# Spectra taken back one slot later, and an output projection in whole tiles with split operands

## The chip, the cores and the metric

The kernel runs on one core of a Trainium2 chip. The metric is the device time of one execution in microseconds (us), as the median of several runs. TensorE is called PE here, its weight loads PEld, VectorE DVE, ScalarE ACT, GpSimd POOL and SyncE SP. All transfers between memory and the core's buffers are issued from SP.

## What is computed

Two layers work on 2048 positions of 448 channels, and their results stand side by side in the output.

```python
# left half: a long convolution per channel (S4D), done with Fourier transforms
dt = exp(log_dt);  A = -exp(log_A_real) + 1j * A_imag;  C = (C_real + 1j * C_imag) * dt[:, None]
P = exp((A * dt[:, None])[:, :, None] * arange(L)[None, None, :])      # D x N x L, N = 256
K = 2.0 * einsum("dn,dnl->dl", C, P).real
y = irfft(rfft(u_t, 2 * L) * rfft(K, 2 * L))[:, :, :L];  a = y.T + u * D_skip
# right half: full attention, 16 heads of 28 channels
q, k, v = split(x @ wqkv)
b = (softmax(q @ k.T * 28 ** -0.5) @ v).reshape(S, D) @ wo
out = concatenate([a, b], axis=-1)
```

## The kernel before, in words

**Attention.** The 16 heads lie in four groups of four heads, and the 2048 queries in four blocks of 512. A unit is one group and one block, so there are 16 units, numbered 0 to 15; units 12 to 15 are the last group. A unit walks over 16 blocks of 128 keys. Each of these 256 pairs (unit u, key block kt) is one step `s` of the main loop (line 1006). For each step there are four score matmuls (`s_mm`: PE writes `pss`, ACT writes the exponentials `p`), four times two column-tiled matmuls with the values of the step before (`pv_step`, tile `po`) and, as long as there is a unit one ahead, four matmuls for the row maxima of that unit (`max_mm`, reduced on DVE). The row maxima end 19 steps before the loop does.

**Order of the work.** `ORDER` (line 34) writes out the order within a step: maximum and score matmuls, then a slot `f`, the value matmuls `pv`, a second slot `f`, and the rest of the maximum and score matmuls. All engines keep program order from here on (line 864), so an instruction that waits holds up all that is behind it on its engine. From step 238 on, each step has a third slot at its end. After the loop there are only slots, two to a step number.

**Slots.** `slot` (line 957) hands each slot to the first that is due: the sums, the scaling and the row maxima of a unit (`urgent`), output projections (`p_due`), matmuls of the convolution kernel (`m_due`), transforms of the input (`u_due`), and otherwise the jobs of the convolution's end (`f_slot`). From step 256 on spectra go ahead of projections. The jobs are:

- 16 spectra (`spectrum`, line 776; halves f = 0 and 1, eight each). Tasks: `forth(0)`; `forth(1)` with two products on DVE each and then `join(0)`, `join(1)`, four sums and differences on POOL, tile `p`; `back(0)` and `back(1)`, PE matmuls on `p`, followed by a copy on ACT and a store `z`. `back(0)` may come only `GAP` slots after `forth(1)`. One spectrum runs at a time; the next one's data (`mw`, `yk`, `uh`) are loaded when one begins.
- 8 pieces of finish (`finish`, line 819; four per half, after all spectra of that half). A load of `zi` and `ut`, a product on POOL, and four matmul groups with an addition on DVE (`one`), stored in pairs.

The second half of the spectra waits until the convolution kernel is done (step 200, lines 1013 to 1017), when the memory and a PSUM bank of that work are given to the ring of four `pm` tiles that all slots use. The first slots of the spectra lie at step 195.

**End of a unit.** `fin` (line 734) copies `po` to `o`, and slots for the row sums (`sums`) and for the scaling follow two and four slots later. In `scale`, PE spreads the reciprocals and DVE multiplies into `on`. For units 0 to 11 `on` is stored (`on_d`); for 12 to 15 four projections of 128 queries each become due, one per step, from two steps after `fin` on. `project` multiplies the four groups' outputs by Wo in float32 through `mm32`, which cuts a 128-column weight into four column tiles of 32; a float32 matmul is two records in the trace. The outputs of the first three groups come as `og` in one load at kt = 12 of the unit (line 1018). Wo lies in two tiles that take both buffers named `ua` (`load_wo`, line 704), so rows that show `pm<-ua,og` and `pm<-ua,on` are projections. ACT copies the result to `y`, which is stored. Rows `pm<-yk,mw` are forth, `pm<-p,mw` back, `p<-pr,pr` join, `pm<-zi,wb` finish.

Every record of the trace carries line 75, the helper through which all instructions are issued, so groups are told apart by their tiles. Matmul operands of type float32r go through PE as one record with whole tiles. Queries, keys and the value projection use that type already, with each operand split into a high part (a rounding copy on ACT) and a rest (a subtraction).

Of the kernel before, what the change touches and what calls it, by code (L numbers as in the profile page):

```python
# [8 lines left out]
F32 = mybir.dt.float32  # L9
F32R = mybir.dt.float32r  # L10
I32 = mybir.dt.int32
AF = mybir.ActivationFunctionType
ALU = mybir.AluOpType
# [5 lines left out]
D = 448  # L19
# [3 lines left out]
G = 4  # L23
HG = H // G
CQ = 512
NQ = L // CQ
# [4 lines left out]
NU = G * NQ  # L31
# [2 lines left out]
ORDER = ('m0', 's0', 'm1', 's1', 'v', 'f', 'pv', 'f', 'v', 'k', 'm2', 's2', 'm3', 's3', 'v')  # L34
PB = 8
F1 = 2
FX, PD, GAP = 1, 2, 2
FL = {"s": 2, "f": 3}
S0, SP, SW, SD, PW, E3 = 0, 4, 0, 5, 37, 8
UG = (2, 2, 4)  # L40
# [50 lines left out]
def body(ctx, tc, a, out):  # L91
    nc = Engines(tc)
# [4 lines left out]
    def pool(stack, name, bufs=1, space=None, side=None):  # L97
        kw = {} if space is None else {"space": space}
        if side:
            kw["side"] = side  # L100
        return stack.enter_context(tc.tile_pool(name=name, bufs=bufs, reuse_waits="tile", **kw))
# [11 lines left out]
    on_d = [dram.tile([G, 128, CQ], F32, name=f"on_{c}") for c in range(NQ)]  # L113
# [11 lines left out]
    def w_tile():  # L125

        n_ring[0] += 1
        return ps_w[0].tile([128, CQ], F32, name=f"pm{n_ring[0] % ps_w[1]}")
# [7 lines left out]
    def mm32(o, w, x_, start, stop, at=0):  # L136

        for i in range(w.shape[-1] // 32):
            c = slice(32 * i, 32 * i + 32)
            nc.tensor.matmul(o[c], w[:, c], x_, start=start, stop=stop, tile_position=(0, at + 32 * i))  # L140
# [4 lines left out]
    def load_k(g, j, p):  # L145
        if j == 0:
            t = k0_t if g == 0 else p.tile([128, HG, L], F32R, name="khat")
            kt_g[g] = [t[:, i] for i in range(HG)]
        for r in range(4):
            nc.sync.dma_start(kt_g[g][j][32 * r:32 * r + 32, :].bitcast(F32), k_d[g][r % 2, 32 * j:32 * j + 32, :])  # L150
# [3 lines left out]
    def load_v(g, c):  # L154
        v_g[g, c] = t = v_p.tile([128, NK // NQ, HG, 32], F32, name="v", bufs=5)
        nc.sync.dma_start(t.rearrange("p t h e -> p t (h e)"), v_d[c][:, g])

    def load_kd(g, j, rows=range(4)):
        if 0 in rows:
            kd_g[g, j] = kd_p.tile([128, CQ], F32R, name=f"kdif{j}")  # L160
        t = kd_g[g, j]
        for r in rows:
            nc.sync.dma_start(t[32 * r:32 * r + 32].bitcast(F32), kd_d[g][r % 2, 32 * j:32 * j + 32, :])

    def load_q(u, rows=range(4)):
        g, c = divmod(u, NQ)
        if 0 in rows:
            q_u[u] = q_p.tile([128, HG, CQ], F32R, name="qhat", bufs=3)
        t = q_u[u]
        for r in rows:  # L170
            nc.sync.dma_start(t[32 * r:32 * r + 32].bitcast(F32), q_d[g][c][r // 2].rearrange("(j p) q -> p j q", j=HG))
# [40 lines left out]
    with ExitStack() as st:  # L212
# [47 lines left out]
        t = a["A_log_dt"]  # L260
# [10 lines left out]
        for k in range(NCK):  # L271
            for s in (1, 0):
                src = wns[k][:, s, :].rearrange("p (g h e) -> p g h e", g=G, e=DH)
                hi, lo = (w_g[:, i, s, k, :, :, :DH] for i in range(2))
# [280 lines left out]
    kq_p = pool(kq_st, "kq_p")  # L555
# [146 lines left out]
    wo_t = []  # L702
# [11 lines left out]
    def s_mm(u, kt, j):  # L714
        pss = ps_s.tile([128, CQ], F32, name="pss")
        nc.tensor.matmul(pss, kt_g[u // NQ][j][:, kt * 128:(kt + 1) * 128], q_u[u][:, j, :], start=True, stop=True)
        p = kq_p.tile([128, CQ], F32, name="p", bufs=PB)
        nc.scalar.activation(p, pss, AF.Exp, scale=SCALE)
        return p
# [5 lines left out]
            nc.tensor.matmul(o_u[u][32 * j:32 * j + 32, :], v_g[u // NQ, kt // NQ][:, kt % NQ, j, :], ps[j],  # L725
                             start=kt == 0, stop=kt == NK - 1, tile_position=(0, 32 * j))

    og_u = {}

    def load_og(u):  # L730
        og_u[u] = og = kq_p.tile([128, G - 1, CQ], F32, name="og")
        nc.sync.dma_start(og, on_d[u % NQ][:G - 1].rearrange("g p q -> p g q"))

    def fin(u, s_):
        g, c = divmod(u, NQ)
        o = kq_p.tile([128, CQ], F32, name="o")
        nc.scalar.activation(o, o_u[u], AF.Copy)
        on = kq_p.tile([128, CQ], F32, name="on", bufs=2)
        rb = kq_p.tile([128, 4, HG, 32], F32, name="rb")
        og = og_u.pop(u, None)  # L740

        def sums():
            pw = w_tile()
            for t in range(4):
                mm32(pw[:, t * HG:(t + 1) * HG], o[:, t * 128:(t + 1) * 128], sel, start=True, stop=True)
            r = kq_p.tile([128, 4, HG], F32, name="r", bufs=2)
            nc.vector.reciprocal(r, pw[:, :4 * HG].rearrange("p (t h) -> p t h", h=HG))
            nc.scalar.activation(rb, r[:, :, :, None].to_broadcast([128, 4, HG, 32]), AF.Copy)

        def scale():  # L750
            pw = w_tile()
            for t in range(4):
                mm32(pw[:, t * 128:(t + 1) * 128], rb[:, t].rearrange("p h e -> p (h e)"), ident, True, True)
            nc.vector.tensor_tensor(on, o, pw, ALU.mult)
            if g < G - 1:
                nc.sync.dma_start(on_d[c][g], on)
            else:
                p_due.extend((s_ + PD + PS * t, lambda t=t: project(t)) for t in range(4))

        def project(t):  # L760
            pw = w_tile()
            ts = slice(t * 128, (t + 1) * 128)
            for g2 in range(G):
                mm32(pw[:, :D], og[:, g2, ts] if g2 < G - 1 else on[:, ts], wo_t[g2 // 2][:, g2 % 2, :],
                     start=g2 == 0, stop=g2 == G - 1)
            y = kq_p.tile([128, D], F32, name="y", bufs=2)
            nc.scalar.activation(y, pw[:, :D], AF.Copy)
            q0 = c * CQ + t * 128
            nc.sync.dma_start(out[q0:q0 + 128, D:], y)

        soon_slot(UG[1], sums)
        soon_slot(UG[2], scale)

    fk = {}
# [130 lines left out]
    f0_st, f1_st = ExitStack(), ExitStack()  # L905
    f_p, f_ready = {}, {}
# [43 lines left out]
    def soon_slot(gap, f):  # L950
        n_urgent[0] += 1
        urgent.append((n_slot[0] + gap, n_urgent[0], f))
        q = sorted(urgent)
        urgent.clear()
        urgent.extend(q)
# [45 lines left out]
    def vec():  # L1001
        if powers["g"]:
            powers["g"].popleft()()

    prev = None
    for s in range(NS):
        u, kt = divmod(s, NK)
        sm = s + NK + LEAD
        if s == 12 * NK:
            k0_st.close()  # L1010
            f_p["s", 0] = f_p["s", 1] = pool(f0_st, "f0_p", side="right")
            f_ready["s", 0], f_ready["s", 1] = s, NS
        if s >= 12 * NK and f_ready["s", 1] == NS and not (k_due or m_due or powers["g"] or powers["e"]):
            g_st.close()
            ps_st.close()
            ps_w[:] = pool(ps_st, "ps_f", 4, PSUM), 1
            f_ready["s", 1] = s + F1
        if kt == 12 and u // NQ == G - 1:
            load_og(u)
        late[0] = s + NK + LEAD > NS  # L1020
        if u % NQ == NQ - 1 and u < NU - 1 and kt % 4 == 2:
            load_v(u // NQ + 1, kt // 4)
        if sm < NS and sm // NK % NQ == NQ - 1 and sm % NK % 4 == 0 and sm % NK and sm // (NQ * NK) + 1 < G:
            load_kd(sm // (NQ * NK) + 1, sm % NK // 4 - 1)
        if sm < NS and sm % (NQ * NK) == 0 and sm:
            load_kd(sm // (NQ * NK), HG - 1)
        if kt % 4 == 1 and u % NQ == 1 and u // NQ + 1 < G:
            load_k(u // NQ + 1, kt // 4, k_pools[(u // NQ + 1) % 2])
        if kt == 2:
            if u + 2 < NU:  # L1030
                load_q(u + 2)
        ps = []
        for op in ORDER:
            if op[0] == "s":
                ps.append(s_mm(u, kt, int(op[1])))
            elif op[0] == "f":
                slot(s)
            elif op[0] == "v":
                vec()
            elif op == "k":  # L1040
                k_next()
                k_begin(s)
                k_seed(s)
                for _ in range(3):
                    if powers["e"]:
                        powers["e"].popleft()()
            elif op == "pv":
                if prev:
                    pv_step(*prev)
                    if prev[1] == NK - 1:  # L1050
                        fin(prev[0], s)
            elif sm < NS:
                max_mm(sm // NK, sm % NK, int(op[1]))
        for _ in range(FX if late[0] else 0):
            slot(s)
        if sm < NS and sm % NK == NK - 1:
            def end(un=sm // NK):
                max_end(un, w_tile())
                max_put(un)
            max_join(sm // NK)  # L1060
            soon_slot(UG[0], end)
        k_next()
        prev = (u, kt, ps)
    pv_step(*prev)
    fin(prev[0], NS)
    s = NS
# [63 lines left out]
```

## Time and profile before

| | us |
|---|---|
| median of 3 runs | 1319.46 |
| lowest and highest | 1316.6, 1322.87 |
| profiled execution | 1316.79 |
| its span, first to last instruction | 1315.1 |
| PE busy | 1229.7 |
| DVE, ACT, POOL busy | 948.6, 953.0, 870.4 |

Mean granted PE clock over the span is 0.98 of full speed. Unit 12 begins at step 192, and the last values' matmul of the loop is at 1292.9 us. In rows of time order the first number is the start in us from the span's start, the second the duration, then engine, line, operation, written tile, read tiles, shape and count; brackets hold the idle time before and what ended it. In lists of waits the numbers are the total in us, the times, and the longest. In rows of groups they are the count, then busy us and mean ns of one, then idle time before. A list of transfers gives their count and KB each.

### The profile page before, as it was taken

How to read it: one execution, taken by the hardware profiler on the slowest of the kernel's cores; microseconds unless marked ns; L12 is line 12 of the kernel's file. 1: busy time of each engine (PE TensorE's matmuls, PEld its weight loads, DVE VectorE, ACT ScalarE, POOL GpSimd, SP SyncE). 2: the span in 40 equal slices, each digit the busy share in tenths (PEclk: the TensorE clock that was granted, in tenths of full speed). 3: DMA queues.
4: the chain of work that ended last, by engine and by line, in shares of the span. 5: the costliest groups of instructions: out<-in, count | busy, mean ns of one | idle time of the engine just before them, and what ended most of it. 6: DMA issues, size and time to landing. Idle time of an engine off the chain costs nothing.

```text
span 1315.1 us, 33199 instructions
## 1 busy us (share of the span) xinstructions
PE 1229.7 (94%) x12625; PEld 698.8 (53%) x12625; DVE 948.6 (72%) x2106; ACT 953.0 (72%) x2068; POOL 870.4 (66%) x736
## 2 busy tenths in 40 slices
PE   6879985899999999999999999999999899999897
PEld 4657763455555555555555555555555444544333
DVE  5898887878777777778778888888887545645111
ACT  4876762488888888888788888888887656646453
POOL 3686681398887788887779999989993414423311
PEclk9989987899999999999999999999999999999999
DMA  6677769736765546468633233732416553925485
GB/s 190 206 276 260 242 205 285 220 73 143 179 147 132 129 136 175 131 174 224 167 100 87 61 78 90 161 80 70 101 37 175 178 158 132 284 87 186 132 219 137
DMA packets 200087, 205.35 MB, mean 156 GB/s; under 512 B 95992, under 2 KB 158520, under 8 KB 197880
## 3 DMA queue, kind: packets, MB, share of 16 engines
q1 hardware_dynamic: 199928, 203.23, 55.9%
q8 instruction: 100, 1.64, 0.5%
q14 instruction: 59, 0.48, 0.1%
HBM read 120.73 MB, written 82.18 MB: 154 GB/s over the span
## 4 chain that ended last, share of the span: by engine, by line
PE 71%; DVE 9%; POOL 7%; DMA 5%; ACT 4%; issue 4%; SPq 0%; ACTq 0%; POOLq 0%; DVEq 0%
PE pm L75 40%; PE pss L75 16%; PE po L75 15%; POOL p L75 2%; DMA k<-hl 2%; DVE tri L75 2%; POOL e L75 1%; DVE mx L75 1%; POOL qhat L75 1%; DVE sg L75 1%; ACT tri L75 1%; DVE px L75 1%; DVE qhat L75 1%; DMA khat<-k 1%; ACT p L75 1%
## 5 line engine op out<-in xcount | busy, mean ns | idle before, releaser
L75 ACT ACTIVATE p<-pss 128x512 f32<-128x512 f32 x1024 | 560.9, 610 | 112.3 <-PE pss L75 109.1
L75 DVE TENSOR_REDUCE mx<-pm 128x1 f32<-128x512 f32 x500 | 321.7, 684 | 125.5 <-PE pm L75 123.4
L75 PE MATMUL pss<-qhat,khat 128*128 128x512 f32 x1024 | 403.3, 400 | 2.3 <-ACT p L75 2.3
L75 PE MATMUL pm<-khat,qhat 128*128 128x512 f32 x749 | 327.1, 440 | 3.4 <-DVE mx L75 2.3
L75 POOL TENSOR_TENSOR e<-e,sdb 128x256 f32<-128x256 f32 x168 | 202.1, 1203 | 118.4 <-ACT e L75 63.1
L75 PE MATMUL po<-p,v 128*32 128x512 f32 x2048 | 269.8, 595 | 0.0
L75 POOL TENSOR_TENSOR e<-e,eu 128x256 f32<-128x256 f32 x168 | 248.3, 1478 | 13.2
L75 PEld LDWEIGHTS pm<-khat,qhat 128*128 128x128 f32 x749 | 141.9, 190 | 197.3 <-ACT p L75 41.9
L75 DVE CUSTOM_DVE_ANT_0 rl<-pm,rl 128x512 f32<-128x512 f32 x249 | 171.5, 689 | 64.8 <-ACT rl L75 61.8
L75 PEld LDWEIGHTS pss<-qhat,khat 128*128 128x128 f32 x1024 | 191.1, 189 | 49.0 <-issue 12.2
L75 POOL TENSOR_TENSOR eu<-e,sdb 128x256 f32<-128x256 f32 x168 | 202.3, 1204 | 0.0
L75 POOL TENSOR_TENSOR p<-pr,pr 64x448 f32<-64x448 f32 x64 | 73.0, 1141 | 149.6 <-PE pm L75 128.6
L75 ACT ACTIVATE rl<-pm 128x512 f32<-128x512 f32 x249 | 150.8, 606 | 20.9 <-PE pm L75 20.9
L75 DVE TENSOR_TENSOR g<-g,zg 128x128 f32<-128x128 f32 x392 | 162.1, 414 | 3.4
L75 PE MATMUL pm<-xh,khat 112*128 112x512 f32 x256 | 90.6, 436 | 21.8 <-DVE hl L75 10.5
L75 PE MATMUL pm<-kdif,qhat 128*128 128x512 f32 x249 | 101.3, 407 | 2.4 <-DMA v<-v 1.3
L75 DVE TENSOR_TENSOR zg<-g,zg 128x128 f32<-128x128 f32 x224 | 87.9, 393 | 5.0
L75 PEld LDWEIGHTS pm<-e,g 128*32 128x32 f32 x3584 | 57.2, 109 | 43.8 <-issue 17.0
L75 ACT ACTIVATE y<-pm 128x448 f32<-128x448 f32 x48 | 26.4, 549 | 73.1 <-PE pm L75 37.7
L75 PE MATMUL pm<-e,g 128*32 128x64 f32 x3584 | 73.1, 222 | 1.9 <-POOL e L75 1.9
L75 PEld LDWEIGHTS pm<-xh,khat 112*128 112x128 f32 x256 | 52.0, 208 | 37.8 <-DVE hl L75 12.9
L75 ACT ACTIVATE ub<-pm 128x224 f32<-128x224 f32 (+1 forms) x96 | 38.8, 449 | 40.0 <-PE pm L75 38.1
(134 smaller groups left out, 1468.7 us busy)
## 6 DMA issues: line engine op xcount, KB each, us to landing
sdb<-sd SPq DMA_DIRECT2D x56, 336.0 KB
khat<-k SPq DMA_DIRECT2D x64, 256.0 KB
qhat<-q SPq DMA_DIRECT2D x64, 256.0 KB
sd<-sg SPq DMA_DIRECT2D x8, 1456.0 KB
k<-hl SPq DMA_DIRECT2D x16, 512.0 KB
q<-hl SPq DMA_DIRECT2D x16, 512.0 KB
mw<-in_mw SPq DMA_DIRECT2D x16, 512.0 KB
sd<-qhat SPq DMA_DIRECT2D x8, 896.0 KB
```

Of the source, the lines that this page charges most:

```text
L75: i = f(*args, **kw)
```

## The change

`GAP` goes from 2 to 3, so that `back(0)` comes at the earliest three slots after `forth(1)`.

The projection becomes 12 float32r matmuls on whole tiles, three per group of heads: high part by high part, high part of o by rest of Wo, and rest of o by high part of Wo. `split` makes a high part with a copy on ACT and a rest with a subtraction. Wo's four parts are split one per step, beginning with the third step after the convolution kernel's end (steps 203 to 206). The other groups' outputs of a block come in three loads, at kt = 11, 12 and 14, into the two buffers `ua` (those in which Wo lies at first), and are split at kt = 13, 14 and 15. The rests are made on POOL. The unit's own output is split after the scaling, its rest on POOL, for the last unit on DVE. The scaled output is written over `o` instead of into `on`. The split parts lie in a pool of their own, in memory that the convolution kernel's work leaves free.

```diff
-FX, PD, GAP = 1, 2, 2
+FX, PD, GAP = 1, 2, 3
...
-    def load_og(u):
-        og_u[u] = og = kq_p.tile([128, G - 1, CQ], F32, name="og")
-        nc.sync.dma_start(og, on_d[u % NQ][:G - 1].rearrange("g p q -> p g q"))
+    def wh_open():
+        wh["p"] = pool(f1_st, "wh_p")
+        wh["w"] = wh["p"].tile([128, 2, G, D], F32R, name="wh")
+        w_due.extend(range(G))
+
+    def split(hi, lo, x_, e):
+        nc.scalar.activation(hi, x_, AF.Copy)
+        e.tensor_tensor(lo, x_, hi.bitcast(F32), ALU.subtract)
+
+    def split_wo(g2):
+        split(wh["w"][:, 0, g2], wh["w"][:, 1, g2], wo_t[g2 // 2][:, g2 % 2, :], nc.gpsimd)
+
+    def load_og(u, g2):
+        og_t[u, g2] = t = kq_p.tile([128, 2 * D], F32, name="ua", bufs=2)
+        nc.sync.dma_start(t[:, :CQ], on_d[u % NQ][g2])
+
+    def split_og(u, g2):
+        if g2 == 0:
+            og_u[u] = wh["p"].tile([128, G - 1, 2, CQ], F32R, name="og")
+        split(og_u[u][:, g2, 0], og_u[u][:, g2, 1], og_t.pop((u, g2))[:, :CQ], nc.gpsimd)
...
-            nc.vector.tensor_tensor(on, o, pw, ALU.mult)
+            nc.vector.tensor_tensor(o, o, pw, ALU.mult)
             if g < G - 1:
-                nc.sync.dma_start(on_d[c][g], on)
+                nc.sync.dma_start(on_d[c][g], o)
             else:
+                wh["on"] = op = wh["p"].tile([128, 2, CQ], F32R, name="op")
+                split(op[:, 0], op[:, 1], o, nc.gpsimd if u < NU - 1 else nc.vector)
                 p_due.extend((s_ + PD + PS * t, lambda t=t: project(t)) for t in range(4))
...
+            n = 0
             for g2 in range(G):
-                mm32(pw[:, :D], og[:, g2, ts] if g2 < G - 1 else on[:, ts], wo_t[g2 // 2][:, g2 % 2, :],
-                     start=g2 == 0, stop=g2 == G - 1)
+                for i, k in ((0, 0), (0, 1), (1, 0)):
+                    x_ = og[:, g2, i, ts] if g2 < G - 1 else wh["on"][:, i, ts]
+                    nc.tensor.matmul(pw[:, :D], x_, wh["w"][:, k, g2], start=n == 0, stop=n == 3 * G - 1)
+                    n += 1
...
-        if kt == 12 and u // NQ == G - 1:
-            load_og(u)
+            wh_open()
+        if w_due and f_ready["s", 1] < s:
+            split_wo(w_due.popleft())
+        if u // NQ == G - 1 and kt >= 11:
+            if kt in (11, 12, 14):
+                load_og(u, (11, 12, 14).index(kt))
+            if kt >= 13:
+                split_og(u, kt - 13)
```

More of the change, by code (lines that the diff above doesn't have):

```diff
@@ L726, in pv_step @@
                              start=kt == 0, stop=kt == NK - 1, tile_position=(0, 32 * j))
-    og_u = {}
-    def load_og(u):
-        og_u[u] = og = kq_p.tile([128, G - 1, CQ], F32, name="og")
-        nc.sync.dma_start(og, on_d[u % NQ][:G - 1].rearrange("g p q -> p g q"))
+    og_u, og_t, wh, w_due = {}, {}, {}, collections.deque()
+    def wh_open():
[14 more added lines that the diff above has]
+        split(og_u[u][:, g2, 0], og_u[u][:, g2, 1], og_t.pop((u, g2))[:, :CQ], nc.gpsimd)
     def fin(u, s_):
@@ L737, in fin @@
         nc.scalar.activation(o, o_u[u], AF.Copy)
-        on = kq_p.tile([128, CQ], F32, name="on", bufs=2)
         rb = kq_p.tile([128, 4, HG, 32], F32, name="rb")
```

## The prediction

> **What bounds the kernel now.** The head of the page comes first, then the busy time by stretches of the last quarter, then its list of waits.
>
> ```profile
> span 1315.1 us, 33199 instructions
> PE 1229.7 (94%) x12625; PEld 698.8 (53%) x12625; DVE 948.6 (72%) x2106; ACT 953.0 (72%) x2068; POOL 870.4 (66%) x736
> ```
>
> TensorE (PE) is busy for 94% of the span. The next table, busy time by stretches, gives per stretch PE, PEld, DVE, ACT and POOL (us, instructions), the granted clock and the DMA share.
>
> ```profile
> 1065.00:1093.00 28.00, 28.00 (x280) 12.93 (x281) 10.72 (x22) 13.55 (x28) 4.58 (x4) 1.00 0.46 137
> 1220.00:1240.00 20.00, 17.95 (x236) 7.68 (x232) 3.56 (x7) 9.75 (x19) 8.25 (x7) 0.91 0.38 104
> ```
>
> 1065 to 1093 holds the four projections of unit 12's block of queries: PE has no idle time at all, and the other engines are at most half busy. There, work taken from PE is time. 1220 to 1240 is different: PE is idle for 2 us, and its clock fell to 0.91. The list of waits from 990 us on says for whom PE waits.
>
> ```profile
> POOL p L75 <- PE pm L75: 128.6, 13, 24.7
> PE pm L75 <- POOL p L75: 14.4, 18, 2.0
> PE pss L75 <- ACT p L75: 2.3, 8, 0.3
> ```
>
> PE lost 14.4 us in 18 waits for POOL's products p, that is back(e) waiting for join(e), and hardly anything for others. POOL itself is idle for long. So the last quarter is bound by PE's work plus a latency through POOL, and the change touches both.
>
> **Part 1: the projection.** One projection of unit 14, in order of time (start, duration), and a piece of finish in the tail:
>
> ```profile
> 1235.85 0.73 PE L75 MATMUL pss<-qhat,khat 128*128 128x512 f32 x2
> 1236.51 2.46 PE L75 MATMUL pm<-ua,og 128*32 128x448 f32 x24
> 1239.54 1.04 PE L75 MATMUL po<-p,v 128*32 128x512 f32 x8
> 1240.40 0.56 PE L75 MATMUL pm<-zi,wb 128*32 128x224 f32 x8
> 1240.89 0.73 PE L75 MATMUL pss<-qhat,khat 128*128 128x512 f32 x2
> ...
> 1299.54 0.56 PE L75 MATMUL pm<-zi,wb 128*32 128x224 f32 x8
> 1299.92 2.44 PE L75 MATMUL pm<-ua,og 128*32 128x448 f32 x24
> ```
>
> From 1236.51 to the po matmuls at 1239.54 a projection takes 3.03 us: 32 records, eight groups of four column tiles. Afterwards it is 12 float32r matmuls of 128x448 on whole tiles. The value projection at the start has that form, with 112 rows instead of 128:
>
> ```profile
> 159.81 0.37 PE L75 MATMUL pm<-vh,xh 112*128 112x448 f32 x1
> ...
> 165.80 0.37 PE L75 MATMUL pm<-vh,xl 112*128 112x448 f32 x1
> ```
>
> There are 30 back to back; 5.99 us over 29 intervals is 0.207 us each, so 2.48 us for 12. The saving is 0.55 us a projection, 16 x 0.55 = 8.8 us, all on the path where PE is full.
>
> The switch between whole tiles and column tiles has a price as well. The second pss of 1235.85 would be through at 1236.32 (two at 0.236 each, the 0.207 above by 512 to 448 columns), yet the column tiles start 0.19 later; the way back at 1240.89 costs some 0.11 (0.49 to the next start, where the same piece takes 0.38 between column tiles at 1299.54). Inside a step a projection stands between pss/pm and po, so the switch only moves to its other side. In the tail it stands among column-tiled work, so each of four gains two switches: 4 x 0.30 = 1.2 us lost (0 to 2). The Trainium skill (TensorEngine Tiling (Array Packing), Key Properties) says that changing the tiling mode drains the engine, which speaks against this edit; the trace agrees, with 0.1 to 0.2 us a change. By a free switch the sum below would be 1.2 us better.
>
> **Part 2: the way back a slot later.** One spectrum now (forth(1), joins on POOL, back(0), po, back(1)), and an empty stretch of the loop:
>
> ```profile
> 1017.65 0.96 PE L75 MATMUL pm<-yk,mw 128*32 128x224 f32 x16 [0.40 <-DVE mx L75]
> 1020.01 4.76 POOL L75 TENSOR_TENSOR p<-pr,pr 64x448 f32<-64x448 f32 x4 [12.37 <-PE pm L75]
> 1022.40 0.96 PE L75 MATMUL pm<-p,mw 128*32 128x224 f32 x16 [0.86 <-POOL p L75]
> 1023.18 1.04 PE L75 MATMUL po<-p,v 128*32 128x512 f32 x8
> 1024.83 0.96 PE L75 MATMUL pm<-p,mw 128*32 128x224 f32 x16 [0.60 <-POOL p L75]
> 1030.28 0.50 PE L75 MATMUL pm<-khat,qhat 128*128 128x512 f32 x1
> 1032.35 1.07 PE L75 MATMUL po<-p,v 128*32 128x512 f32 x8
> ```
>
> From the start of forth(1) it takes 2.36 us until POOL begins and 4.76 us until it ends; back(0) needs the first half (4.7 us), back(1) all of it (7.1 us). Two slots are one step: eight matmuls (2.07 us, 1030.28 to 1032.35), po (0.86 us) and the filled slot (0.8 us), 4 us with the switches. So back(0) comes 0.86 us early, then back(1) 0.60 us. With GAP 3, back(0) is one and a half steps off, 5.6 us or more, and back(1) 7.4 us or more: both waits vanish in the two-slot steps. By the slot rules a spectrum then takes six slots instead of five, the last back moves from step 241 to 247, and the free slots pay, not time. From step 238 on a step has three slots, so GAP 3 is one step there:
>
> ```profile
> 1219.30 0.96 PE L75 MATMUL pm<-p,mw 128*32 128x224 f32 x16 [1.92 <-POOL p L75]
> 1220.08 1.75 PE L75 MATMUL po<-p,v 128*32 128x512 f32 x8
> 1221.73 1.72 PE L75 MATMUL pm<-p,mw 128*32 128x224 f32 x16
> 1223.38 0.86 PE L75 MATMUL pss<-qhat,khat 128*128 128x512 f32 x2
> ```
>
> Here back(0) waited 1.92 us, and the work behind it ran slow: po took 1.65 us to the next start instead of 0.86, back(1) 1.65 instead of 0.78. That is 1.6 us more. By the slot rules spectra 4 and 7 of the second half still wait under GAP 3 (about 0.6 us for each back, their slots stand a step of 4 us apart), so I leave 3 us of the 14.4 (bounds 0 and 6): a gain of 11.4 us, and 1.5 us for the clock (0 to 1.6). The Trainium skill (TensorE: Matmul & The Clock Gate, its section on oscillation) wants idle gaps over about 3.4 us before the clock falls; the row shows slower matmuls after 1.92 us, so the measurement decides. By the page the 1.5 us would not be there.
>
> **Part 3: the splits.** Their instructions by the nearest rows (group, count, busy us, mean ns):
>
> ```profile
> L75 POOL TENSOR_TENSOR vl<-tri,vh 112x448 fp32r<-112x448 f32 x4 | 5.1, 1282 | 12.6 <-ACT vh L75 12.5
> L75 ACT ACTIVATE hl<-pm 128x512 fp32r<-128x512 f32 x16 | 9.5, 593 | 2.5 <-PE pm L75 2.5
> ```
>
> Added are 20 copies on ACT (20 x 0.6 = 12 us), 19 rests on POOL (about 1.3 us for 448 elements, 1.45 for 512; 27 us) and one on DVE. In the stretch above, ACT is busy 13.6 of 28 us and POOL 4.6, so their busy time costs nothing. Their place in the queues does: a copy that waits stands in front of the exponentials p, and after three pss PE stands still.
>
> The worst place is unit 12. Its two loads at steps 203 and 204 need the two "ua" buffers in which Wo lies, and a buffer is free only after both its Wo halves are split, at 204 and at 206. The loads wait on SP's queue, with z stores, the row maxima of unit 13 and spectrum loads behind them. With step 203 at 0: the join of spectrum 2 (counted from 0) holds POOL until 8.1, Wo's second rest ends at 9.4, the load is issued at 9.5 and lands 3 us later, while ACT stands at its copy from 9.5. In step 206 the fourth copy, its rest (1.3) and the second load (3) stand in a row in front of ACT again, 4.4 us. ACT loses 7.4 us, of which PE's lead of three pss hides about 1: **6.5 us** (0 to 12). The landing time is not in the trace for this size; these rows bound it:
>
> ```profile
> 1285.58 0.55 SPq L75 DMA_DIRECT2D zi<-z  x1
> 1286.23 1.31 SPq L75 DMA_DIRECT2D ut<-in_A_u  x2
> 1293.43 2.08 POOL L75 TENSOR_TENSOR ut<-ut,dsk 128x896 f32<-128x896 f32 x1 [4.32 <-DMA ut<-in_A_u]
> zi<-z SPq DMA_DIRECT2D x8, 896.0 KB
> ut<-in_A_u SPq DMA_DIRECT2D x16, 224.0 KB
> ```
>
> 896 + 2 x 224 KB landed 7.85 us after the first issue; 256 KB by size alone would be 1.5 us. I take 3, nearer to the small end, as nothing else is in flight then. In the other units the third load is issued about a step before its copy (4.4 us): 1.5 us together for bad luck (0 to 14).
>
> The last rest of unit 14 stands on POOL behind a join: forth(1) ends at 0, join 1.35 to 6.1, rest to 7.4, while PE wants it at 6.0: 1.4 us (0 to 3). Units 12 and 13 have POOL free there: DVE, copy and rest need 2.8 us, the other nine operands and two more give 2.3 after a pause for po.
>
> **The tail**, after the last step:
>
> ```profile
> 1295.63 1.08 PE L75 MATMUL pm<-ident,rb 128*32 128x128 f32 x32 [1.05 <-ACT rb L75]
> 1296.53 2.44 PE L75 MATMUL pm<-ua,og 128*32 128x448 f32 x24
> 1296.85 0.69 DVE L75 TENSOR_TENSOR on<-o,pm 128x512 f32<-128x512 f32 x1 [1.93 <-PE pm L75]
> ```
>
> The scaled o is ready at 1297.54; copy (0.6) and rest on DVE (0.68) give 1298.9, while PE has its first eleven matmuls done at 1298.8: 0.25 us with the semaphore. Two more pieces of finish (0.38 each) stand here that stood in the loop, so they cancel. Seven empty late steps with 0.28 us of wait for ACT become five: 0.5 us gained.
>
> **Sum**, against the profiled execution (1316.8 us, span 1315.1): -8.8 + 1.2 - 11.4 - 1.5 + 6.5 + 1.5 + 1.4 + 0.25 - 0.5 = -11.35, so 1305.4 us. The median of the runs (1319.5) lies 2.7 us above that execution: 1308.
>
> **Rivals.** First, slower: the loads land late. If 256 KB behind other transfers need 7.85 us, unit 12's two stalls grow by 4.85 each, and the third load of each unit stalls ACT by 3.45 (instead of 1.5 together): 9.7 + 12.3 = 22 us, 1330 us. It decides from a landing of about 6 us on. For it: Wo's buffers and one step of lead. Against: DMA is busy 46% and 38% in the two stretches. Second, no gain from part 2: the rests push the joins back in POOL's queue and back(e) waits as before: 1308 + 12.9 = 1321 us. For it: POOL runs in order, and splits and joins meet in steps 203 to 207, 221 to 223 and 237 to 239. Against: 128.6 us of POOL idle. Third, unit 12's block is hidden by the exponentials' lead and ACT's free half: 1308 - 6.5 = 1301.5 us.
>
> **How the numbers follow.** Forecast 0.61, late loads 0.14, no gain on POOL 0.13, no block 0.12. A measurement of this kernel can tell about 0.5%, 6.6 us, so faster means below 1312.9, slower above 1326. The forecast's unknown terms (block, landing, waits left over) spread it over 1298 to 1319: 0.46 faster, 0.14 same, 0.01 slower. The third rival is faster (0.12). The second is same (0.11) or slower (0.02); the first slower (0.13), same 0.01. That makes 0.58, 0.26, 0.16. The range that leaves out about 2 in 10 is 1297 to 1324: at its top it takes in the second rival.
>
> **What would show it.** The pm matmuls of a projection 12 in 2.5 us. PE's wait for POOL p below 6 us. A wait of ACT for the "ua" load at two steps near 1038 to 1050 us, with PE's pss behind it, 5 to 8 us together, and none over 1 us in later units. The last exponential earlier by some 11 us, the tail unchanged. The forecast is wrong if ACT waits for "ua" in every unit, if PE still waits 10 us for POOL, or if projections take over 2.8 us.

## The result, and the profile after

The changed kernel takes 1306.94 us (median of 6 runs, 1304.93 to 1309.48), beside 1320.41 us before (6 runs, 1316.6 to 1324.67). The ratio is 0.9897, with a 95% interval of 0.9874 to 0.992; in a second set of runs it was 0.9912 (0.9894 to 0.993). The profiled execution took 1309.48 us. The head of its page:

```profile
span 1307.7 us, 32613 instructions
PE 1226.9 (94%) x12305; PEld 721.7 (55%) x12305; DVE 949.6 (73%) x2107; ACT 962.0 (74%) x2088; POOL 894.4 (68%) x755
```

The two profiles are not alike ahead of the change. The first matmul of forth, and the sums of unit 12, as rows of time order, before and then after:

```profile
996.67 0.94 PE L75 MATMUL pm<-yk,mw 128*32 128x224 f32 x16
...
1061.25 0.44 PE L75 MATMUL pm<-sel,o 128*32 128x4 f32 x32
```

```profile
999.07 0.94 PE L75 MATMUL pm<-yk,mw 128*32 128x224 f32 x16
...
1061.35 0.43 PE L75 MATMUL pm<-sel,o 128*32 128x4 f32 x32
```

The profile after reaches the first forth 2.4 us late, and a second profile of the very same kernel reached it at 996.39: the first 1000 us wander by a few us from one execution to the next. So profiles are compared here from that row on, and the last quarter is cut at the first `pm<-sel,o` row of units 12, 13, 14 and 15 and at the end of the span (us; experiments below):

| kernel | to sums 12 | 12 to 13 | 13 to 14 | 14 to 15 | to the end | last quarter |
|---|---|---|---|---|---|---|
| before | 64.58 | 83.53 | 83.74 | 65.63 | 20.95 | 318.43 |
| changed | 62.28 | 74.41 | 75.88 | 74.62 | 21.44 | 308.63 |
| e1: GAP 3 alone | 57.03 | 76.34 | 78.02 | 69.68 | 22.64 | 303.71 |
| e2: projection alone | 68.03 | 82.12 | 81.52 | 65.00 | 20.01 | 316.68 |
| e3: Wo split early | 57.36 | 74.44 | 75.84 | 74.36 | 21.42 | 303.42 |
| e4: all loads early | 57.75 | 74.19 | 75.85 | 70.72 | 22.20 | 300.71 |
| e5: e4, rest 14 on DVE | 57.75 | 74.15 | 75.86 | 69.44 | 22.55 | 299.75 |
| e6: e4, GAP 4 | 55.13 | 72.21 | 71.50 | 74.31 | 33.47 | 306.62 |
| e7: e4, high parts only | 57.75 | 67.75 | 69.43 | 62.26 | 15.69 | 272.88 |
| e8: e4, GAP 2 | 64.88 | 82.26 | 80.79 | 65.40 | 19.79 | 313.12 |
| f3: e5, tail in a row | 57.74 | 74.18 | 75.86 | 68.63 | 22.41 | 298.82 |

With a larger GAP, spectra and finish pieces move from the first columns to the last two, so single columns are compared only between kernels of the same GAP.

The list of waits of the changed kernel from 990 us on, beside the one of before in the prediction:

```profile
PE pss L75 <- ACT p L75: 4.2, 7, 2.3
PE pm L75 <- POOL p L75: 3.2, 6, 0.8
PE pm L75 <- ACT rl L75: 2.6, 1, 2.6
PE pm L75 <- DMA zi<-z: 1.6, 1, 1.6
PE pm L75 <- POOL op L75: 1.1, 1, 1.1
ACT og L75 <- DMA ua<-on: 6.6, 3, 3.1
```

PE's wait for the spectra's products fell from 14.4 to 3.2 us. New are waits behind ACT (2.6 us, and 2.3 of the 4.2), one for a load of finish, and one for unit 14's rest. ACT itself stood 6.6 us at copies whose load had not landed. In order of time, the first of these places:

```profile
1041.14 5.08 SPq L75 DMA_DIRECT2D ua<-on  x2
1043.89 0.63 ACT L75 ACTIVATE og<-ua 128x512 fp32r<-128x512 f32 x1 [3.13 <-DMA ua<-on]
...
1044.60 1.29 POOL L75 TENSOR_TENSOR og<-ua,og 128x512 fp32r<-128x512 f32 x1 [2.38 <-ACT og L75]
...
1045.06 0.50 PE L75 MATMUL pm<-khat,qhat 128*128 128x512 f32 x1 [2.59 <-ACT rl L75]
...
1048.27 1.72 PE L75 MATMUL pm<-yk,mw 128*32 128x224 f32 x16
```

The load issued at 1041.14 landed 2.75 us later, and ACT had waited 3.13 us for it. PE stood 2.59 us. The SP row joins two loads: the second was issued when the first one's rest on POOL had freed its buffer (1044.60 and 1.29 us). The forth at 1048.27 then took 1.49 us to the next start, where the same 16 matmuls otherwise take 0.78. The second place, in the last unit:

```profile
1270.48 0.38 SPq L75 DMA_DIRECT2D zi<-z  x1
...
1275.33 0.55 SPq L75 DMA_DIRECT2D ua<-on  x1
...
1280.96 0.63 ACT L75 ACTIVATE og<-ua 128x512 fp32r<-128x512 f32 x1 [2.69 <-DMA ua<-on]
...
1282.13 0.70 PE L75 MATMUL pss<-qhat,khat 128*128 128x512 f32 x1 [2.32 <-ACT p L75]
1282.76 2.75 PE L75 MATMUL po<-p,v 128*32 128x512 f32 x8
```

The third load was issued at 1275.33, with the 1344 KB of zi and ut ahead of it, and had landed 5.6 us later, when ACT's copy began; ACT waited 2.69 us, PE 2.32, and po behind it took 1.7 us to the next start instead of 0.86. Both places by stretches (PE, PEld, DVE, ACT, POOL busy; then clock, DMA share, GB/s):

```profile
1041.00:1046.00 5.00, 2.41 (x23) 0.86 (x13) 0.93 (x4) 2.11 (x5) 2.51 (x3) 1.00 0.19 52
1046.00:1051.00 5.00, 5.00 (x34) 2.28 (x37) 2.61 (x7) 3.95 (x8) 2.42 (x2) 0.66 0.64 192
1278.00:1282.00 4.00, 1.81 (x10) 0.41 (x10) 0.00 (x0) 1.31 (x4) 0.33 (x1) 1.00 0.94 297
1282.00:1287.00 5.00, 4.65 (x57) 1.97 (x57) 0.63 (x2) 2.14 (x5) 3.29 (x3) 0.66 0.69 155
```

In the 5 us behind each, the mean granted clock was 0.66. In slices of 1 us it was 0.87, 0.50, 0.50, 0.50 and 0.92 from 1046 on: half of full speed for some 3.4 us, which is 1.7 us of lost work. A wait of this length need not bring it: in f1, a second profile of the same kernel, PE stood nearly as long at the first place, and every slice behind it kept the full clock:

```profile
1042.23 0.50 PE L75 MATMUL pm<-khat,qhat 128*128 128x512 f32 x1 [2.43 <-ACT rl L75]
```

A projection in the loop, and one in the tail:

```profile
1224.91 0.73 PE L75 MATMUL pss<-qhat,khat 128*128 128x512 f32 x2
1225.48 1.98 PE L75 MATMUL pm<-wh,og 128*128 128x448 f32 x9
1227.30 0.78 PE L75 MATMUL pm<-wh,op 128*128 128x448 f32 x3
1228.01 1.07 PE L75 MATMUL po<-p,v 128*32 128x512 f32 x8
...
1291.48 0.59 PE L75 MATMUL pm<-zi,wb 128*32 128x224 f32 x8
1292.00 2.08 PE L75 MATMUL pm<-wh,og 128*128 128x448 f32 x9
1293.92 0.77 PE L75 MATMUL pm<-wh,op 128*128 128x448 f32 x3
1294.62 0.58 PE L75 MATMUL pm<-zi,wb 128*32 128x224 f32 x8
```

From 1225.48 to 1228.01 it is 2.53 us, against 3.03 before. In the tail a projection with its piece takes 3.14 us (1291.48 to 1294.62) where it took 3.38.

### The profile page after: what moved, and what is told of

Same layout as the page of the kernel before. It is cut to its first block, busy times and chain, and to the rows that moved or that the text cites. A ratio compares the mean times of both kernels' runs of the same rounds, so it can differ in the third digit from the quotient of the medians.

```text
span 1307.7 us, 32613 instructions
## 1 busy us (share of the span) xinstructions
PE 1226.9 (94%) x12305; PEld 721.7 (55%) x12305; DVE 949.6 (73%) x2107; ACT 962.0 (74%) x2088; POOL 894.4 (68%) x755
## 4 chain that ended last, share of the span: by engine, by line
PE 71%; DVE 11%; POOL 6%; DMA 4%; ACT 4%; issue 3%; SPq 1%; ACTq 0%; POOLq 0%; DVEq 0%
PE pm L75 40%; PE pss L75 16%; PE po L75 15%; DVE tri L75 2%; DVE mx L75 2%; POOL e L75 1%; POOL qhat L75 1%; POOL p L75 1%; DVE qhat L75 1%; ACT tri L75 1%; DVE sg L75 1%; DVE rl L75 1%; DMA qhat<-q 1%; DMA tri<-in_B_wqkv 1%; DVE px L75 1%
## 5 line engine op out<-in xcount | busy, mean ns | idle before, releaser
L75 PE MATMUL pm<-xh,khat 112*128 112x512 f32 x256 | 94.2, 452 | 23.5 <-DVE hl L75 11.0
L75 PEld LDWEIGHTS pm<-e,g 128*32 128x32 f32 x3584 | 57.2, 109 | 43.7 <-issue 16.1
L75 DVE TENSOR_TENSOR pr<-pm,ub 128x448 f32<-128x448 f32 x64 | 37.0, 619 | 54.3 <-PE pm L75 41.1
```

What stands on the lines that cost most here:

```text
L75: i = f(*args, **kw)
```

## The experiments

**e1 and f2, GAP 3 alone.** The kernel before with one number changed; f2 is the same kernel, run again beside f1.

```diff
-FX, PD, GAP = 1, 2, 2
+FX, PD, GAP = 1, 2, 3
```

> Only GAP 3, the projection left as before. Theory (the terms of the sum each hold by themselves): PE's wait for POOL p falls from 14.4 us to about 3 and the clock keeps up, so 12 to 13 us faster than before, about 1308 us where before stands at 1320. Rival (the slots only move work into the tail, and the cheaper projection made the whole gain): less than 4 us faster, 1316 or more.

Measured: 1303.97 us beside 1318.85, ratio 0.9886 (0.9874 to 0.9899); the last quarter is 14.7 us shorter. Its waits:

```profile
PE pm L75 <- POOL p L75: 2.7, 4, 0.8
PE pss L75 <- ACT p L75: 1.4, 5, 0.3
```

The theory holds, and the way back is worth more than was forecast: 11.7 us less waiting for POOL, 0.9 less for ACT, and no low clock behind the late waits (about 1.7). The rival is out, and by the last quarters this alone is worth more than the whole change (14.7 us against 9.8).

**e2, the projection alone.** The changed kernel with GAP 2.

```diff
-FX, PD, GAP = 1, 2, 3
+FX, PD, GAP = 1, 2, 2
```

> The whole changed kernel but with GAP 2. Theory: 8 us are gained on PE's path by the projections, and given back by two places where ACT waits for a load (about 4 us each, half of it idle time of PE and half a lower clock behind it) and 1.1 us at unit 14: within 3 us of before, 1318 to 1322. Rival (the waits for loads are hidden, as PE has other idle time anyway): 6 to 9 us faster, 1311 to 1314.

Measured: 1315.91 us beside 1318.85, ratio 0.9976 (0.9965 to 0.9987); the last quarter is 1.75 us shorter. The stretches between sums show 1.4 and 2.2 us gained per four projections, and the first stretch 3.45 us lost, where Wo is split. The time is what the theory said, and its rival is out; but its second block, in the last unit, did not come. With GAP 2 the loads of finish lie at other steps there. At unit 12 no low clock follows, and PE is seen to wait only 0.8 us for ACT and 1.3 us, in four waits, for DVE. A low clock came elsewhere: behind both late waits for POOL (1.91 and 2.04 us), where in the profile of before only the first had one.

**f1, the changed kernel again, beside f2.** No edit; the question is what the projection's part is worth beside GAP 3, on one chip.

> The changed kernel as it is, beside the next two on one chip. Theory: the blocks of units 12 and 15 eat what the projections gain beyond the way back, so it is slower than GAP 3 alone by 3 to 5 us (last quarter 308.6 against 303.7 us). Rival (the order on different chips was chance): it is faster than GAP 3 alone, by up to 5 us.

> GAP 3 alone, beside the changed kernel on one chip. Theory: about 1304 us where before stands at 1319, ratio 0.987 to 0.990. Rival: slower than the changed kernel.

Measured: 1307.02 us for the changed kernel and 1303.33 for GAP 3 alone, ratios 0.9912 (0.9894 to 0.993) and 0.9886 (0.9867 to 0.9904). The intervals overlap a little, but the order is that of the first set, and the last quarters are 308.0 and 303.75 us in this pair, 308.6 and 303.7 in the first. So beside GAP 3, the projection's part of the change costs about 4 us.

**e3, Wo split earlier.** One part a step as in the change, from step 200 on.

```diff
-        if w_due and f_ready["s", 1] < s:
+        if w_due:
             split_wo(w_due.popleft())
```

> The changed kernel with Wo split from step 200 on instead of 203, one part per step as before, so that both ua buffers are free before the loads of steps 203 and 204. Theory: the idle time of 2.6 us at 1042 and the low clock behind it go, 4 us faster than the changed kernel, about 1303. Rival (PE would have waited there for something else): the same as the changed kernel, 1307.

Measured: 1300.98 us, ratio 0.9867 (0.9853 to 0.9881). The first stretch falls from 62.28 to 57.36 us, all other stretches stay within 0.3 us of the changed kernel's. So the block at unit 12 costs 4.9 us, or 4.4 beside f1, more than the 2.6 and 2.4 us that PE is seen to wait there. The low clock isn't needed for that: f1 had none, and its two steps at the block took 7.00 and 5.00 us from po to po, against 3.82 and 3.80 in e3. In the second of them PE waits twice for DVE; what else makes up the rest is not shown. The block of the last unit is still there, as PE's wait of 3.05 us for ACT.

**e4, all loads with three steps of lead.**

```diff
-        if w_due and f_ready["s", 1] < s:
+        for _ in range(2 if w_due else 0):
             split_wo(w_due.popleft())
-        if u // NQ == G - 1 and kt >= 11:
-            if kt in (11, 12, 14):
-                load_og(u, (11, 12, 14).index(kt))
-            if kt >= 13:
-                split_og(u, kt - 13)
+        if u // NQ == G - 1 and kt >= 8:
+            if kt in (8, 9, 12):
+                load_og(u, (8, 9, 12).index(kt))
+            if kt in (11, 12, 15):
+                split_og(u, (11, 12, 15).index(kt))
```

> The changed kernel with Wo split two parts a step from step 200 on, and the three loads of a unit at kt 8, 9 and 12 with their splits at 11, 12 and 15, so that each load has three steps before its split. Theory: both blocks go, 8 us faster than the changed kernel, about 1299; no wait of ACT for the ua load over 0.5 us. Rival (the block at the loop's end is the transfers of zi and ut, which hold up any load there): the block in the last unit stays, 1303.

Measured: 1300.89 us, ratio 0.9857 (0.9842 to 0.9873). The last quarter is 7.9 us shorter than the changed kernel's (8 expected), 4.5 of it in the first stretch and 3.9 in that of the last unit, and ACT has no wait for `ua` left. The median stands less far below, 1300.9 instead of 1299, and no lower than e3's; the first 1000 us move single runs by more than that. What PE still waits for:

```profile
PE pm L75 <- POOL p L75: 3.3, 6, 0.8
PE pm L75 <- DMA zi<-z: 1.2, 1, 1.2
PE pm L75 <- POOL op L75: 1.1, 1, 1.1
PE pm L75 <- DVE op L75: 0.9, 1, 0.9
```

Beside e1 the stretches 12 to 13 and 13 to 14 are each 2.2 us shorter, 0.54 a projection, which is the 0.55 of the forecast. From 14 to 15 it is 1.0 us longer instead: the waits for zi and for op, unit 14's split output, are new there. The wait for zi is not a matter of a shorter lead. The rows of the changed kernel, and the same piece of finish in e1, whose load was issued at 1255.22:

```profile
1255.49 0.36 SPq L75 DMA_DIRECT2D zi<-z  x1
...
1262.27 0.59 PE L75 MATMUL pm<-zi,wb 128*32 128x224 f32 x8 [1.58 <-DMA zi<-z]
```

```profile
1260.46 0.59 PE L75 MATMUL pm<-zi,wb 128*32 128x224 f32 x8
```

In both PE wants the tile 5.2 us after the load's issue. In e1 it was there; in the changed kernel it came after 6.8 us.

**e5, unit 14's rest on DVE.** On top of e4:

```diff
-                split(op[:, 0], op[:, 1], o, nc.gpsimd if u < NU - 1 else nc.vector)
+                split(op[:, 0], op[:, 1], o, nc.gpsimd if u < NU - 2 else nc.vector)
```

> The kernel with all loads early, and the rest of unit 14's own output on DVE instead of POOL, where it stands behind a join. Theory: PE's wait of 1.1 us for op at unit 14 goes, so the last quarter takes 299.6 us instead of 300.7, and nothing else moves. Rival (DVE's own queue delays it as much): the wait stays at 1 us under DVE's name.

Measured: 1300.38 us, ratio 0.9859 (0.9835 to 0.9883). The wait at unit 14 is gone and its stretch 1.3 us shorter, the last quarter 299.75 us. The theory holds; in the median it can't be told from e4.

**e6, GAP 4.** On top of e4:

```diff
-FX, PD, GAP = 1, 2, 3
+FX, PD, GAP = 1, 2, 4
```

> The kernel with all loads early, and GAP 4 instead of 3. Theory: in the two-slot steps there is nothing left to hide (waits for POOL p of 0.5 us before step 238), so a fourth slot only moves more spectra and finish pieces towards the end: the last quarter within 3 us of 300.7, and not faster by more than the 1.3 us of waits that are left in the three-slot steps; the tail after the last sums grows from 22 us to 24 or more. Rival (PE's idle time is still hidden in other waits behind the joins): 3 us faster or more.

Measured: 1306.28 us, ratio 0.9909 (0.988 to 0.9937), last quarter 306.62 us. The theory was right that nothing is gained and that the tail grows, but not in the size: 5.9 us lost instead of at most 3, and 33.5 us of tail where it had 24 or more. The line that is new in the list of waits:

```profile
PE pm L75 <- DMA zi<-z: 7.7, 2, 6.5
```

PE now waits for loads of finish, in the tail once for 6.5 us, with a low clock behind it. Slots are free only as long as what moves back still has work in front of it.

**e7, high parts only.** e4 with four of the twelve matmuls: the kernel leaves out the products with the rests.

```diff
-                for i, k in ((0, 0), (0, 1), (1, 0)):
+                for i, k in ((0, 0),):
...
-                    nc.tensor.matmul(pw[:, :D], x_, wh["w"][:, k, g2], start=n == 0, stop=n == 3 * G - 1)
+                    nc.tensor.matmul(pw[:, :D], x_, wh["w"][:, k, g2], start=n == 0, stop=n == G - 1)
```

> The kernel with all loads early, with the high parts' product alone in the projection (4 matmuls instead of 12; the products with the rests are left out, the splits themselves are still made). Theory: where PE is full, 8 matmuls less are 1.65 us a projection, 6.6 us in each of the stretches from the sums of unit 12 to those of 13 and from 13 to 14 (74.2 and 75.9 us become 67.6 and 69.3); from the sums of unit 14 to those of 15 it is less, 3 to 5 us, as the loads of zi and the exponentials set the pace in part of it. Rival (PE is full everywhere): 6.6 us in all three.

Measured: 1272.5 us in one run; the three stretches are 6.4, 6.4 and 8.5 us shorter. The rival comes closer: PE is full from the sums of unit 14 on as well, and there the waits for zi and for unit 14's op (1.2 and 1.1 us in e4) went besides. The first stretch, which has no projection, stayed at 57.75 us. So matmuls taken away are time in every stretch that has projections.

**e8, GAP 2 with the loads early.** On top of e4:

```diff
-FX, PD, GAP = 1, 2, 3
+FX, PD, GAP = 1, 2, 2
```

> The kernel with all loads early, but with GAP 2: the projection's part without its blocks and without the way back's. Theory: the block at unit 12 goes (3.5 us in the first stretch of the kernel with the projection alone) and the rest stays: last quarter 312 us, that is 6 us faster than before, and PE's wait for POOL p stays at 14 to 16 us. Rival (the waits for POOL take over what the projection frees): within 2 us of the projection alone, 316 us.

Measured: 1313.22 us beside 1317.22, ratio 0.9966 (0.9951 to 0.9982), last quarter 313.12 us (312 expected), 5.3 us less than before. The theory holds; PE's wait for POOL p is 16.1 us, 1.7 more than before, so part of what the projections free is lost there. Each part by itself gives 14.7 and 5.3 us, together 20.0; e4 has 17.7. The difference is the size of the two waits that neither part has alone, for zi (1.2 us) and for unit 14's op (1.1). That they are its cause is argued.

**f3, the tail's projections in a row.** e5, with the last unit's projections due half a step apart.

```diff
-                p_due.extend((s_ + PD + PS * t, lambda t=t: project(t)) for t in range(4))
+                p_due.extend((s_ + PD + (PS if u < NU - 1 else 0.5) * t, lambda t=t: project(t)) for t in range(4))
```

> The kernel with all loads early and the rest of unit 14 on DVE, with the four projections of the last unit one after the other instead of each followed by a finish piece. Theory (each change between whole and column tiles costs 0.14 us): three projections less stand between column tiles, six changes less, the last projection ends 2.3 us earlier (three pieces of 0.38 us come after it, 0.14 us for each change) and the tail is 0.8 us shorter, 21.7 instead of 22.5 us. Rival (the pieces of finish are what ends the kernel, with their additions on DVE and their stores): the tail stays, 22.5 us or more.

Measured: 1297.06 us, ratio 0.9842 (0.9823 to 0.9862), the lowest median of the kernels with all twelve matmuls, though its interval overlaps those of e4 and e5; the tail is 22.41 us against 22.55 in e5. The rows of the tail, idle time before each in brackets:

```profile
1275.46 2.10 POOL L75 TENSOR_TENSOR ut<-ut,dsk 128x896 f32<-128x896 f32 x1 [4.34 <-DMA ut<-in_A_u]
1275.78 2.33 DVE L75 TENSOR_TENSOR op<-o,op 128x512 fp32r<-128x512 f32 x1 [0.70 <-ACT op L75]
...
1278.16 0.47 PE L75 MATMUL pm<-wh,op 128*128 128x448 f32 x1 [1.47 <-DVE op L75]
1278.47 1.99 PE L75 MATMUL pm<-wh,og 128*128 128x448 f32 x9
...
1280.90 1.99 PE L75 MATMUL pm<-wh,og 128*128 128x448 f32 x9
...
1285.87 2.48 PE L75 MATMUL pm<-zi,wb 128*32 128x224 f32 x48
```

A projection is 2.43 us from one to the next, against 3.14 with a piece of 0.38 behind it, so two changes of tiling cost 0.33 us. The last projection ends 1.84 us earlier after the sums than in e5 (14.18 against 16.02 us). But the span then goes on for 8.23 us instead of 6.53: six stores at the end are issued one after the other. So the theory had the price of a change and the earlier end of the projections, but not the tail: its gain of 0.14 us, where 0.8 was forecast, is too small to tell, and the rival comes closer. The stretch from 14 to 15, in which nothing was changed, is 0.8 us shorter than in e5, as PE waits 0.5 us for zi instead of 1.3.

## Why the prediction came out right, and where its sum was off

The forecast was 1308 us and the result 1306.9, within the range. That it came so close is luck in part. The way back and the block at unit 12 came out 1.8 and 1.6 us better than forecast, the third loads and a wait that was not foreseen 2.4 and 1.6 us worse, and these nearly cancel. By the last quarters the change gained 9.8 us (10.4 in f1), where the sum has 11.35.

- **PE's work as the bound.** Right, and shown by e7: taking matmuls away shortens every stretch that has projections.
- **Projection, 0.55 us each.** Right: 2.53 for 3.03 us in the rows, 0.54 each between e1 and e4 in units 12 and 13. The tail's loss by changes of tiling was right too: 0.30 us a projection forecast, 0.33 in f3. Of the whole saving less is left in the last quarter: 5.3 us with GAP 2 (e8), 3.0 with GAP 3 (e4 against e1).
- **Way back, 11.4 and 1.5 us.** The mechanism was right: the waits vanish in two-slot steps but for 0.2 us, 3.2 us stay (3 forecast), 2.8 of them at spectra 4 and 7 of the second half as forecast, and free slots pay. The size was too small: alone it gave 14.7 us, for 12.9 forecast. The waits in e1 account for 12.6 and the late clock for about 1.7.
- **Block at unit 12, 6.5 us.** Right in place and cause, Wo's buffers, as e3 shows by freeing them: 4.9 us. The load landed in 2.75 us (3 forecast). The way to PE was another: it stood not at the scores, for p, but at the row maxima, for ACT's copy rl, which waits behind the same copy. I had put the cost on such idle time alone. 2.6 us were that; the low clock, which I had not counted, was there in one of two profiles, and the rest is not taken apart. ACT's two waits came to 4.0 us; the sign had named 5 to 8. The second stop, at step 206, was 0.83 us of ACT instead of 4.4, because the second load did not wait for Wo's second buffer, as I had it, but took the one that the first load's rest freed at 1045.89, and came in while ACT caught up.
- **Third loads, 1.5 us together.** This step failed. It took the step ahead of the copy as 4.4 us in every unit. In the last unit an empty late step is 2.6 us long (po at 1275.63 to po at 1278.27), and zi and ut stand ahead of the load, which needed 5.6 us. That cost 3.9 us (e4): 2.3 of idle time, and a low clock. e4 gives the load more lead and another place in the queue at once, so how much each does is open. The sign that no later unit has a wait of ACT over 1 us failed with it: it was 2.69. The slower rival named this mechanism with a landing of 7.85 us in every unit; units 13 and 14 had none of it, so the rival was right in one unit of four.
- **Unit 14's rest, 1.4 us.** Right: 1.1 us of wait, and e5 takes 1.3 us off.
- **Not foreseen:** PE's wait for zi (1.6 us). The lead from issue to use is the same as in e1 (5.2 us), so shorter steps are not the reason: the load lands later. With that lead, 5.2 to 5.3 us, the wait was nothing in e1 and e7, 0.3 us in f2, and 0.5 to 1.6 us in the kernels with GAP 3 and the whole projection. Why it lands later there stays open.

Taken together, the projection's side of my sum cost 1.6 us net (-8.8 + 1.2 + 6.5 + 1.5 + 1.4 + 0.25 - 0.5). Beside GAP 3 it cost some 4 us (f1 against f2), and without its blocks it gains 3 (e4 against e1). What stays open is why the changed kernel's medians gained 13.5 and 11.6 us where its profiles' last quarters show 9.8 and 10.4: the stretch ahead of the change wanders by more than that difference, but no run separates it.

## What to carry to other kernels

When a step is moved or a buffer is reused, write down for each new load who must free its buffer, what is queued ahead of it, and how long a step is at that very place; a lead counted in steps shrinks where steps get short, and the same lead in time can be enough in one kernel and too short in the next. Put a waiting copy on an engine only if nothing that feeds the bound engine stands behind it. And try the parts of a change apart: here one number carried the whole gain, and the larger edit paid only once its loads were early.

## What the runs showed of the hardware

PE's granted clock fell to half for some 3.4 us behind idle times of 2.6 and 2.3 us in the changed kernel and of 1.92 us in the kernel before. The sum over the 1-us slices is 1.7 us of lost work each time. But f1's 2.43 us had no such cost, nor, in the profile of before, in order of time, an idle time of 2.04 us:

```profile
1231.66 0.96 PE L75 MATMUL pm<-p,mw 128*32 128x224 f32 x16 [2.04 <-POOL p L75]
1232.44 1.04 PE L75 MATMUL po<-p,v 128*32 128x512 f32 x8
```

The 16 matmuls took 0.78 us to the next start, full pace; in e2 the same two waits of before, 1.91 and 2.04 us, were both followed by the half clock. So a wait of PE of some 2 us can cost 1.7 us on top, but need not, and no run here shows what decides.

A subtraction of two 128x512 operands on DVE took 0.69 us in the changed kernel (1290.34) and 2.33 us in f3, while POOL worked on a product of two operands from 1275.46 to 1277.56 beside it. In e4 and e5 the same pair met, with 1.75 and 2.05 us. In all three the subtraction ended 0.55 us after the product, however long before its end it had begun. The Trainium skill (GPSIMD Engine Reference, Specifications) says that DVE and POOL share their way to the buffer memory and contend when a DVE instruction has two inputs there; the runs agree. It cost PE 0.9 to 1.5 us in the last unit, so a rest on DVE is not safe from POOL.
